# Output projection in one-tile steps, and a new order of all steps, in a two-branch attention and convolution kernel

## The chip, the cores and the metric

The kernel runs on one core of one Trainium2 chip. The time is device microseconds of one launch. TensorE (PE) does the matmuls, VectorE (DVE) and ScalarE (ACT) the elementwise work and the copies out of PSUM, GpSimd (POOL) tables and a few DMAs, and SyncE (SP) issues nearly all DMAs, in the order of the program.

## The reference, cut to what matters

Two independent branches over 2048 positions and 576 channels, joined along the last axis. A is attention with 32 heads of 18 channels, in which each position sees itself and seven earlier ones at distances 2, 4 up to 14, followed by a projection with `wo`. B is a short convolution of `k`, a product with `v`, a long causal convolution by FFT, and a product with `q`.

```python
qkv = (x @ wqkv).reshape(B, S, 3, H, Dh)          # A
logits = einsum("bhsd,bhswd->bhsw", q, kg) * scale # kg: k at s, s-2 ... s-14
o = einsum("bhsw,bhswd->bhsd", softmax(logits), vg)
a = o.reshape(B, S, D) @ wo
kv = (sum of 4 shifted k * shift_k) * v            # B
y = irfft(rfft(kv, 2 * S) * rfft(ssm_k, 2 * S))[:S] + kv * ssm_D
b = q * y
return concatenate([a, b], axis=-1)
```

## The kernel before

All work is cut into small steps, and a string `ORDER` lists them: the program issues them in exactly this order, and each engine works off its instructions in this order. An entry is a step's name with its indices. After a colon, "a" or "b" picks the PSUM pool of the step and "v" or "s" the engine that copies its result out of PSUM (DVE, L104, or ACT, L102; ACT if nothing is said). Each of the two pools has two tiles of two banks, so four tiles are in flight.

Branch A: `lx` loads x (L237), `xt` transposes it (L371), `lwq` and `lwt` load the weights, `qk` and `qt` project to q and k (L377), `lm` multiplies q by a shifted k on DVE (L493, L497), `lb` sums the products over a head (L502 to L510), `sm` is the softmax in seven parts per half of the positions, 0 to 6: maxima (L524 to L528), subtraction (L530), exp on ACT (L532), sum on PE (L536) with its logarithm and exp on ACT, normalising product (L540). `sp` spreads the result over partitions by DMA (L546), `v` projects to v (L384), `vh` copies its halo, `pm` multiplies v by the weights on DVE (L600), `ps` sums the products on PE (L610). `lwo` loads `wo` (L271), `po` is the output projection (L622, store L631), and `pz` a projection step that also holds the last two sums.

Branch B: `lk`, `lv`, `lkn`, `ld` are loads, `cv` the parts of the short convolution on DVE (L455 to L468), `kt` transposes the long filter (L481), `sx` and `kp` are the first FFT stage of the data and of the filter (L432), whose results go to DRAM (L439). `xl` and `kl` load them back in another layout (L559) into a ring of four slots; `xs` and `ks` are the second stage (L553), each with two PSUM tiles of one pool and two copies. `gp` multiplies the spectra on DVE (L575), `gi` is the first inverse stage (L588), stored to DRAM by POOL (L593). `yl` loads that (L649, the same ring), `ql` loads q (L653), `ys` is the last stage (L662) with the product by q on DVE (L666), and the result is stored (L668). `ia`, `ib`, `im` and the `t` entries make tables, `sk` and `wt` spread or reorder weights.

One `po.hv.r.di` takes a quarter of the positions' rows and half of the output columns. It holds two PSUM tiles, one of each pool, for the two blocks `e` of 128 positions; 36 matmuls alternate between them, and two copies and two stores follow.

Of the kernel before, what the change touches and what calls it, by code (L numbers as in the profile page):

```python
# [23 lines left out]
kp.7.1:a qk.0.0.1:b cv.1.0 cv.0.7 cv.1.5 kp.7.2:a cv.1.1 cv.2.3 sx.0.0:b kt.3:as qk.0.1.2:b wt:v cv.1.2 sx.0.1:av
cv.1.6 sx.0.2:b qt.1:a sx.1.0:b sx.1.1:b qk.1.0.1:a lv.2 sx.1.2:b kp.5.0:a qt.3:b qk.1.1.0:a cv.2.1 cv.1.7 cv.2.4
cv.3.1 cv.2.0 qt.2:a kp.5.1:b cv.3.4 kp.5.2:bv qk.0.1.1:a ia.5 cv.2.2 sx.2.0:av sx.2.1:b sx.2.2:bv lv.3 kt.0:as
sx.3.0:a sx.3.1:b cv.2.5 qk.1.1.1:b sx.3.2:a kp.3.0:a qk.1.1.2:b cv.3.3 kp.3.1:a ia.4 qt.0:b ib cv.2.6 cv.3.5 kp.3.2:a
ia.7 kt.4:bs cv.3.0 qk.1.0.2:a cv.3.2 kp.0.0:b cv.3.6 cv.2.7 kp.0.1:b cv.3.7 ia.2 kp.0.2:a kt.6:as lm.0.1 lm.0.2 ia.1
qk.0.0.3:b sx.4.0:a sx.4.1:b sx.4.2:a v.6:b lm.0.0 lm.1.0 lb.0:a ia.0 lm.1.1 sx.5.0:b sx.5.1:b lm.6.1 lm.6.2 sx.5.2:a
v.0:a lb.1:a sx.6.0:b sx.6.1:b vz sx.6.2:a lm.6.0 lm.7.1 ia.3 v.7:a lm.2.2 sx.7.0:b sx.7.1:a lb.6:b sx.7.2:a lm.7.0  # L30
v.8:b kp.4.0:a lm.2.0 kp.4.1:b lb.7:b lm.2.1 lm.3.0 kp.6.0:a xl.5 xl.2 kp.4.2:a kp.6.1:b v.2:b kp.6.2:a lb.2:a lm.3.1
lm.4.0 xs.5.0:b kl.2 xs.5.1:a kl.5 v.5:b lb.3:a lm.4.2 lm.4.1 xs.2.0:b im.1 v.1:a xs.2.1:b lm.5.0 lb.4:a lm.5.1
# [16 lines left out]
def kernel(  # L49
# [50 lines left out]
    def evac(dst, src, scale=None, on="s"):  # L100
        if (how["ev"] or on) == "s":
            nc.scalar.activation(dst, src, ACT.Copy, **({} if scale is None else {"scale": scale}))  # L102
# [455 lines left out]
    def w_load(Dd, key, i):  # L558
        nc.sync.dma_start(Wr.get((key, i)), by_rt(Dd, i // 4, i % 4))  # L559
# [65 lines left out]
    def p_fin(pss, hv, r, di):  # L625
        d0, d1 = DCH[di]
        for e in range(2):
            stage = sAr.get((hv, r, di, e))
            evac(stage, pss[e][:, :, 0:HD])
            a = 4 * (2 * r + e) + 2 * hv  # L630
            nc.sync.dma_start(outt[:, a:a + 2, d0:d1], stage)  # L631
            sAr.drop((hv, r, di, e))
# [82 lines left out]
```

## Time and profile before

| what | value |
|---|---|
| runs | 207.99, 210.42, 212.53 us, median 210.42 |
| profiled execution | 207.84 us, span 205.8 us |
| mean granted TensorE clock | 0.996 |
| PE busy, instructions | 189.4 us (92%), 2250 |
| DVE busy, instructions | 181.8 us (88%), 159 |
| ACT busy, instructions | 163.9 us (80%), 249 |
| all copies by ACT from psA and psB | 82.6 and 84.5 us, 237 of them |

How to read the profile. Times are microseconds, unless marked ns. The profile shows one execution; the span runs from its first to its last instruction, and the execution's own time is a little longer. PE is TensorE's matmuls, PEld its weight loads, SPq the issuing of DMAs by SyncE. L12 is line 12 of the kernel. In a timeline each row has the start, the duration from the first instruction's start to the last one's end, the engine, the line, the operation with its output and input, and the count; in brackets stands how long the engine was idle before it and what ended the wait. PEclk is the granted clock as a share of the full one. "psA" and "psB" are the two PSUM pools, "area" any of the SBUF areas.

The busy digits of the page, in 40 slices of the span, in tenths:

```profile
PE   7899989999999999999988897888999999999991
PEld 2564455544544666656746654556676777786871
DVE  6866999999999799999999997999999988994370
ACT  3799566999879988788798999989999995452352
```

Every engine is close to full from about 20 us on; ACT and DVE thin out in the last sixth.

### The profile page before, as it was taken

The numbers are of one execution on the slowest core, as the hardware profiler recorded it, in microseconds if no ns is written. First come the engines' busy times: TensorE is split into PE (matmuls) and PEld (weight loads), VectorE is DVE, ScalarE is ACT, GpSimd is POOL, SyncE is SP. The second block draws the span as 40 slices with busy tenths as digits, with TensorE's granted clock in tenths as the row PEclk, the third lists the DMA queues.
The fourth block names the chain that finished last, engine by engine and source line by source line (L and its number), as shares of the span: only waits on it lengthen the run. The fifth ranks groups of instructions, "written<-read, shape, count | busy, mean of one in ns | idle before, by whom it ended". The sixth has DMA issues, their size and how long they took to land.

```text
span 205.8 us, 5415 instructions
## 1 busy us (share of the span) xinstructions
PE 189.4 (92%) x2250; PEld 123.4 (60%) x2257; DVE 181.8 (88%) x159; ACT 163.9 (80%) x249; POOL 12.5 (6%) x39
## 2 busy tenths in 40 slices
PE   7899989999999999999988897888999999999991
PEld 2564455544544666656746654556676777786871
DVE  6866999999999799999999997999999988994370
ACT  3799566999879988788798999989999995452352
POOL 8300000000000000000020021001001011000000
PEclk9999999999999999999999999999999999999998
DMA  5999998876586874559897679999586998999866
GB/s 151 341 349 244 422 394 270 216 210 205 141 259 149 234 186 122 140 151 350 248 292 252 212 196 273 331 349 380 200 270 227 283 255 289 296 335 268 264 185 202
DMA packets 55162, 52.17 MB, mean 254 GB/s; under 512 B 7073, under 2 KB 49762, under 8 KB 55138
## 3 DMA queue, kind: packets, MB, share of 16 engines
q1 hardware_dynamic: 53888, 47.09, 76.8%
q0 software_dynamic: 1248, 4.74, 6.0%
q8 instruction: 17, 0.28, 0.6%
q14 instruction: 7, 0.06, 0.1%
q10 hardware_dynamic: 2, 0.00, 0.0%
HBM read 29.71 MB, written 18.87 MB: 236 GB/s over the span
## 4 chain that ended last, share of the span: by engine, by line
PE 48%; ACT 20%; DMA 14%; DVE 9%; issue 4%; SPq 3%; ACTq 1%; DVEq 0%
ACT area L102 19%; PE psB L384 6%; PE psA L622 5%; PE psB L622 4%; DMA area<-in_B_k_dram 4%; PE psB L610 4%; PE psA L384 3%; DMA area<-in_B_ssm_k_dram 3%; PE psA L377 3%; PE psB L377 3%; PE psB L432 3%; DMA area<-in_A_x_dram 3%; PE psA L432 2%; DMA Dx<-area 2%; DVE area L104 2%
## 5 line engine op out<-in xcount | busy, mean ns | idle before, releaser
L102 ACT ACTIVATE area<-psA 128x576 bf16<-128x576 f32 (+8 forms) x118 | 82.6, 739 | 25.6 <-PE psA L622 8.3
L102 ACT ACTIVATE area<-psB 128x576 bf16<-128x576 f32 (+6 forms) x119 | 84.5, 752 | 9.4 <-PE psB L384 3.2
L600 DVE TENSOR_TENSOR area<-area,area 128x4096 bf16<-128x4096 bf16 x18 | 40.6, 2286 | 0.7 <-DMA area<-area 0.6
L493 DVE TENSOR_TENSOR area<-area 128x4096 bf16<-128x4096 bf16 x16 | 35.6, 2283 | 1.0 <-ACT area L102 1.0
L377 PEld LDWEIGHTS <-area 128*128 128x128 bf16 x160 | 15.6, 98 | 17.1 <-issue 0.2
L461 DVE TENSOR_TENSOR area<-area,area 128x2304 bf16<-128x2304 bf16 x16 | 21.1, 1351 | 1.6 <-DMA area<-in_B_k_dram 1.6
L575 DVE TENSOR_TENSOR area<-area 128x2304 bf16<-128x2304 bf16 x16 | 21.5, 1352 | 1.0 <-PE psB L553 0.8
L553 PEld LDWEIGHTS <-W 128*64 128x64 bf16 x256 | 13.7, 108 | 11.9 <-issue 10.1
L384 PEld LDWEIGHTS <-area 128*64 128x64 bf16 x180 | 17.6, 193 | 3.4 <-issue 2.3
L377 PE MATMUL psA<-area,area 128*128 128x512 bf16 x78 | 18.5, 379 | 0.2
L377 PE MATMUL psB<-area,area 128*128 128x512 bf16 x77 | 18.4, 379 | 0.2
L622 PE MATMUL psA<-area,area 64*128 64x288 bf16 x144 | 18.0, 283 | 0.4 <-ACT area L102 0.4
L622 PE MATMUL psB<-area,area 64*128 64x288 bf16 x144 | 17.9, 283 | 0.0
L610 PEld LDWEIGHTS <-ident 64*64 64x64 bf16 x576 | 15.2, 106 | 3.2 <-issue 2.8
L588 PEld LDWEIGHTS <-IAt 64*128 64x128 bf16 x256 | 12.5, 94 | 7.5 <-issue 3.7
L622 PEld LDWEIGHTS <-area 64*128 64x128 bf16 x288 | 14.2, 94 | 4.5 <-issue 0.9
L553 PE MATMUL psB<-area,W 128*64 128x288 bf16 x136 | 13.0, 291 | 3.4 <-ACT area L102 2.0
L455 DVE TENSOR_TENSOR area<-area,area 128x2304 bf16<-128x2304 bf16 x11 | 14.8, 1352 | 0.1
L432 PEld LDWEIGHTS <-T 128*128 128x128 bf16 x96 | 8.5, 98 | 9.7 <-issue 3.4
L610 PE MATMUL psB<-area,ident 64*64 64x256 bf16 x384 | 12.4, 271 | 0.2
L384 PE MATMUL psB<-area,area 128*64 128x512 bf16 x100 | 12.2, 388 | 0.2
L432 PE MATMUL psA<-area,T 128*128 128x384 bf16 x52 | 11.9, 327 | 0.2 <-DVE area L363 0.2
(114 smaller groups left out, 212.6 us busy)
## 6 DMA issues: line engine op xcount, KB each, us to landing
Dk<-area SPq DMA_DIRECT2D x16, 288.0 KB, 3.4
Dx<-area SPq DMA_DIRECT2D x16, 288.0 KB, 3.1
area<-Dx SPq DMA_DIRECT2D x8, 576.0 KB, 6.4
area<-Dk SPq DMA_DIRECT2D x8, 576.0 KB, 5.3
Dy<-area POOLq DMA_DIRECT2D x8, 576.0 KB, 5.3
area<-Dy SPq DMA_DIRECT2D x8, 576.0 KB, 5.7
area<-in_A_x_dram SPq DMA_DIRECT2D x8, 288.0 KB, 5.6
area<-in_B_k_dram SPq DMA_DIRECT2D x4, 576.0 KB, 8.0
```

The lines of the kernel that those rows point to most:

```text
L102: nc.scalar.activation(dst, src, ACT.Copy, **({} if scale is None else {"scale": scale}))
L377: nc.tensor.matmul(ps[:, u, :], w[:, kb, cols[u]:cols[u] + 128], xT[:, j, kb], start=(kb == 0), stop=(kb == 4))
L384: nc.tensor.matmul(ps[64 * s:64 * s + 64, aa, :], wv[:, kb, n:D:9], xT[:, 2 * s + aa, kb], start=(kb == 0), stop=(kb == 4), tile_position= ...
L432: nc.tensor.matmul(ps[:, ri, 0:384], T1[:, ri, :], sf[:, 384 * ch:384 * ch + 384], start=True, stop=not extra)
L455: nc.vector.tensor_tensor(dst, dst, src, ALU.add)
L461: nc.vector.tensor_tensor(dst, kfull[:, 4 * c + 3 - j:4 * c + 7 - j, :], skb[:, j, :].unsqueeze(1).to_broadcast([128, 4, D]), ALU.mult)
L493: nc.vector.tensor_tensor(prr.get((n, h)), q2[h], k2[h][:, :, o0:o0 + S], ALU.mult)
L553: nc.tensor.matmul(ps[64 * hp:64 * hp + 64, im, 0:HD], W2[:, im, 8 * g + 2 * prl + hp].rearrange("p l f -> p (l f)"), Wt[:, 2 * prl + hp, ...
L575: nc.vector.tensor_tensor(Pv, Xv.unsqueeze(2).to_broadcast([128, 2, 2, 2 * HD]), Kv.unsqueeze(1).to_broadcast([128, 2, 2, 2 * HD]), ALU.mult)
L600: nc.vector.tensor_tensor(Pr.get((hv, p)), vv, L2[:, hv].rearrange("p a n t -> p n a t"), ALU.mult)
L610: nc.tensor.matmul(ps[64 * b:64 * b + 64, r, 0:256], ident[g, g], P[g, n, :, 128 * b:128 * b + 128], start=(n == 0), stop=(n == W - 1), ti ...
L622: nc.tensor.matmul(pss[e][:, b, 0:HD], Os[hv][g, i, r, 128 * e:128 * e + 128], w[g, d0:d1], start=(i == 0), stop=(i == 8), tile_position=( ...
```

## The change

A projection step now has one tile: a fourth index `e` names the block of 128 positions, and the step has 18 matmuls, one copy and one store. `pz` still has two tiles, but now does the seven first products of one tile before those of the other, and finishes one tile before it starts the last two products of the other.

```diff
-    def p_acc(pss, hv, r, di, lo, hi):
+    def p_acc(ps, hv, r, di, e, lo, hi):
         d0, d1 = DCH[di]
         for i in range(lo, hi):
             w = wos[0][:, i] if i < 3 else wos[1][:, i - 3]
-            for e in range(2):
-                for b in range(2):
-                    g = slice(64 * b, 64 * b + 64)
-                    nc.tensor.matmul(pss[e][:, b, 0:HD], Os[hv][g, i, r, 128 * e:128 * e + 128], w[g, d0:d1],
-                                     start=(i == 0), stop=(i == 8), tile_position=(64 * b, 0))
+            for b in range(2):
+                g = slice(64 * b, 64 * b + 64)
+                nc.tensor.matmul(ps[:, b, 0:HD], Os[hv][g, i, r, 128 * e:128 * e + 128], w[g, d0:d1],
+                                 start=(i == 0), stop=(i == 8), tile_position=(64 * b, 0))
...
-    def p_out(hv, r, di):
-        pss = [psum("a", 2, 512), psum("b", 2, 512)]
-        p_acc(pss, hv, r, di, 0, 9)
-        p_fin(pss, hv, r, di)
+    def p_out(hv, r, di, e):
+        ps = psum("b" if e else "a", 2, 512)
+        p_acc(ps, hv, r, di, e, 0, 9)
+        p_fin(ps, hv, r, di, e)

     def p_tail(hv, r, di):
         pss = [psum("a", 2, 512), psum("b", 2, 512)]
-        p_acc(pss, hv, r, di, 0, 7)
+        for e in range(2):
+            p_acc(pss[e], hv, r, di, e, 0, 7)
         p_sum(hv, 7, psum("a", 2, 512), "s")
         p_sum(hv, 8, psum("b", 2, 512), "v")
-        p_acc(pss, hv, r, di, 7, 9)
-        p_fin(pss, hv, r, di)
+        for e in range(2):
+            p_acc(pss[e], hv, r, di, e, 7, 9)
+            p_fin(pss[e], hv, r, di, e)
```

The order is new from the first entry to the last, with new choices of pool and copying engine. The stretches that matter here are the loads at the start, the middle around the softmax and the end:

```diff
-lwt lx.3.0 lx.3.1 tj t0 wm.11:a lx.0.0 t2 lx.2.0 tv xt.3.2:a sk.2:a sk.1:b lx.2.1 xt.3.1:bs sk.0:b xt.3.0:bs xt.2.2:as
...
-ks.2.0:b xl.1 ks.2.1:a ks.5.0:b lb.5:a gp.2.0 sm.0.0 sm.0.1 sm.0.2 sm.0.3 ks.5.1:b xl.3 gp.2.1 vh.0 sm.1.0 sm.1.1 kl.3
-gi.2.0:b kl.1 ql.0 ql.2 sm.0.4 v.4:a ql.1 sm.0.5:a sm.1.2 sm.1.3 sm.0.6 vh.2 v.3:bv sm.1.4 ql.3 ks.1.0:a gp.5.0 sp.0.0
-lwo.1 sp.0.1 gi.2.1:b xs.1.0:a im.0:v sm.1.5:b ks.1.1:b gp.5.1 vh.1 gi.5.0:a xl.0 sm.1.6 xs.1.1:b gi.5.1:a gp.1.0
...
-ys.2.1:bs ql.5 yl.6 yl.4 ps.0.0:a ys.0.0:a ys.0.1:b yl.7 ys.3.1:a po.0.0.0 po.0.1.1 po.0.1.0 ql.7 yl.5 ql.6 pm.1.2
-pm.1.6 pm.1.1 ps.1.6:b pm.1.8 ps.1.2:a pm.1.7 ps.1.1:b po.0.0.1:v pz.1.0.0:s ys.7.0:as po.1.0.1:v po.1.1.1 ys.4.0:b
-ys.4.1:as ys.6.0:as ys.7.1:b ys.5.0:as ys.5.1:b ys.6.1:a po.1.1.0
+lx.1.0 lx.1.1 lx.2.0 lx.3.0 lx.3.1 lx.2.1 tj wm.11:b t0 t2 xt.1.2:as xt.1.1:bs xt.1.0:as xt.3.1:as t3 lwt lwq.1.0 t1
+lx.0.0 lx.0.1 xt.2.1:b tv xt.2.2:bs xt.2.0:as qk.1.0.1:a lwq.0.1 lwq.0.0 lwq.1.1 xt.0.2:b lk.0 xt.0.0:b xt.3.0:as
...
+xs.2.0:b lm.3.1 lm.4.0 lm.4.2 im.0 v.1:a xs.5.0:b lb.3:a lm.4.1 xs.2.1:b v.4:a vh.0 lm.5.0 lb.4:a lm.5.1 xs.5.1:a kl.5
+ks.2.0:b ks.2.1:a lb.5:b gp.2.0 xl.7 ks.5.0:a xl.1 vh.2 gi.2.0:b gp.2.1 xs.1.0:a sm.0.0 sm.0.1 ks.5.1:b sm.0.2 xl.3
+sm.0.3 sm.0.4 sm.1.0 ql.2 xs.1.1:av ql.0 sm.1.1 kl.1 kl.3 ql.3 gi.2.1:b sm.1.2 sm.1.3 sm.0.5:a ks.1.0:b sm.0.6 gp.5.0
+v.3:av sp.0.0 sm.1.4 gp.1.0 lwo.1 ks.1.1:b sm.1.5:a sp.0.1 gi.5.0:a gp.5.1 sm.1.6 gi.1.0:b gp.1.1 vh.1 xs.3.0:b
+ks.3.0:a kl.0 sp.1.0 gi.5.1:b gp.3.0 xs.3.1:a ks.3.1:a pm.0.5 xl.0 kl.4 pm.0.6 gi.1.1:b gp.3.1 ks.0.0:a pm.0.7
...
+gp.4.1 yl.2 po.0.0.0.0:b yl.0 po.0.0.1.0:a gi.4.0:b pm.1.1 po.0.1.0.0:av gi.4.1:b pm.1.2 po.0.1.0.1:a gp.6.1 ys.3.0:bs
+ys.3.1:bs ys.1.0:as ys.1.1:as ql.4 ps.1.1:b ps.1.6:a gi.6.1:bv po.0.0.1.1:a po.0.1.1.0:b pm.1.4 po.0.1.1.1:b pm.1.5
+ys.2.0:as ys.0.0:as ql.7 yl.6 ys.0.1:b ys.2.1:as ps.1.2:a ps.1.4:a ps.1.5:a po.0.0.0.1:b pm.1.7 ql.6 yl.5 yl.7 pm.1.8
+yl.4 ql.5 pz.1.0.0:s po.1.0.1.0:a po.1.1.0.1:av po.1.1.1.0:av ys.6.0:b ys.6.1:as ys.7.0:a ys.7.1:bs ys.5.0:a ys.5.1:bs
+ys.4.0:b ys.4.1:a po.1.1.1.1:bv po.1.1.0.0:a po.1.0.1.1:b
```

Copies now marked for DVE are sk.0, kp.7.1, sx.0.0, kp.5.0, kp.0.0, xs.1.1, v.3, gi.6.1 and four projection pieces; before they were qk.0.0.2, kp.2.2, sx.0.1, kp.5.2, sx.2.0, sx.2.2, v.3, wt, im.0 and two projection steps of two copies.

More of the change, by code (lines that the diff above doesn't have):

```diff
@@ L24 @@
[L24 to L32, printed above, removed]
-ks.2.0:b xl.1 ks.2.1:a ks.5.0:b lb.5:a gp.2.0 sm.0.0 sm.0.1 sm.0.2 sm.0.3 ks.5.1:b xl.3 gp.2.1 vh.0 sm.1.0 sm.1.1 kl.3
@@ new lines @@
+cv.0.5 kt.2:bs kp.1.0:b kp.1.1:a lv.1 kp.1.2:a t5 qk.0.0.1:b kt.7:b kp.2.0:a kp.2.1:a kp.2.2:b kt.5:bs cv.0.6 cv.1.1
+qk.1.0.2:a cv.0.7 kp.7.0:b kp.7.1:av lwv cv.1.5 cv.2.3 ld cv.1.2 qk.0.1.0:b kp.7.2:b qk.1.1.0:a ia.5 sx.0.0:bv kt.3:as
+cv.2.1 sx.0.1:b sx.0.2:a cv.1.6 qk.0.0.0:b kp.5.0:av qt.3:b cv.3.3 kp.5.1:a cv.3.1 kp.5.2:a cv.3.4 cv.1.7 lv.3 cv.3.5
+qk.1.1.3:b sx.1.0:a sx.1.1:b sx.1.2:a ia.4 qk.1.1.2:b cv.3.0 sx.2.0:a cv.2.4 sx.2.1:b cv.3.2 qk.1.1.1:a cv.2.5
+sx.2.2:b sx.3.0:a qk.0.1.2:b lv.2 cv.3.6 kt.0:a sx.3.1:b cv.3.7 qt.1:a sx.3.2:b kp.3.0:b ia.3 qk.1.0.0:a kp.3.1:a
@@ new lines @@
+kp.3.2:b cv.2.0 qk.0.0.3:b cv.2.2 vz ia.1 cv.2.6 ia.6 cv.2.7 kt.6:a kp.0.0:bv kp.0.1:a kp.0.2:b kt.4:as lm.0.0 lm.0.2
+lm.0.1 v.7:b lm.6.2 im.1 ib lm.1.0 ia.7 v.2:a ia.0 sx.4.0:a sx.4.1:b lb.0:b sx.4.2:a sx.5.0:a v.0:b lm.1.1 sx.5.1:b
+sx.5.2:a lb.1:b sx.6.0:a lm.6.0 lm.6.1 sx.6.1:b sx.6.2:b v.6:a lm.7.1 sx.7.0:b sx.7.1:a sx.7.2:a lm.2.2 lb.6:b lm.7.0
+kp.4.0:a xl.2 kp.4.1:a lm.2.0 v.5:b lb.7:a lm.2.1 kp.4.2:b kp.6.0:b xl.5 kp.6.1:a lm.3.0 v.8:b lb.2:a kp.6.2:a kl.2
+xs.2.0:b lm.3.1 lm.4.0 lm.4.2 im.0 v.1:a xs.5.0:b lb.3:a lm.4.1 xs.2.1:b v.4:a vh.0 lm.5.0 lb.4:a lm.5.1 xs.5.1:a kl.5
@@ new lines @@
+pm.0.8 sp.1.1 xl.6 gi.3.1:b gp.0.1 ks.7.0:a pm.0.3 gi.0.0:b ks.7.1:a gp.7.0 xl.4 gi.0.1:b lwo.2 ps.0.3:a ks.6.0:b
+ps.0.8:a xs.6.0:b pm.0.0 lwo.0 pm.1.3 xs.6.1:a gi.7.0:b pm.1.0 ps.1.3:a ps.0.0:a gp.7.1 lwo.3 pm.0.2 ks.6.1:b xs.4.0:a
+yl.1 ps.1.0:b pm.0.1 gi.7.1:a ks.4.0:b xs.4.1:a ps.0.2:b ps.0.1:a ks.4.1:b ql.1 gp.6.0 yl.3 gp.4.0 gi.6.0:a pm.1.6
+gp.4.1 yl.2 po.0.0.0.0:b yl.0 po.0.0.1.0:a gi.4.0:b pm.1.1 po.0.1.0.0:av gi.4.1:b pm.1.2 po.0.1.0.1:a gp.6.1 ys.3.0:bs
+ys.3.1:bs ys.1.0:as ys.1.1:as ql.4 ps.1.1:b ps.1.6:a gi.6.1:bv po.0.0.1.1:a po.0.1.1.0:b pm.1.4 po.0.1.1.1:b pm.1.5
@@ L618, in p_acc, with p_fin @@
             w = wos[0][:, i] if i < 3 else wos[1][:, i - 3]
-            for e in range(2):
-                for b in range(2):
-                    g = slice(64 * b, 64 * b + 64)
-                    nc.tensor.matmul(pss[e][:, b, 0:HD], Os[hv][g, i, r, 128 * e:128 * e + 128], w[g, d0:d1],
-                                     start=(i == 0), stop=(i == 8), tile_position=(64 * b, 0))
-    def p_fin(pss, hv, r, di):
-        d0, d1 = DCH[di]
[L627 to L632, printed above, removed]
-    def p_out(hv, r, di):
-        pss = [psum("a", 2, 512), psum("b", 2, 512)]
-        p_acc(pss, hv, r, di, 0, 9)
-        p_fin(pss, hv, r, di)
+            for b in range(2):
+                g = slice(64 * b, 64 * b + 64)
+                nc.tensor.matmul(ps[:, b, 0:HD], Os[hv][g, i, r, 128 * e:128 * e + 128], w[g, d0:d1],
+                                 start=(i == 0), stop=(i == 8), tile_position=(64 * b, 0))
+    def p_fin(ps, hv, r, di, e):
+        d0, d1 = DCH[di]
+        stage = sAr.get((hv, r, di, e))
+        evac(stage, ps[:, :, 0:HD])
+        a = 4 * (2 * r + e) + 2 * hv
+        nc.sync.dma_start(outt[:, a:a + 2, d0:d1], stage)
+        sAr.drop((hv, r, di, e))
+    def p_out(hv, r, di, e):
+        ps = psum("b" if e else "a", 2, 512)
+        p_acc(ps, hv, r, di, e, 0, 9)
+        p_fin(ps, hv, r, di, e)
     def p_tail(hv, r, di):
         pss = [psum("a", 2, 512), psum("b", 2, 512)]
-        p_acc(pss, hv, r, di, 0, 7)
+        for e in range(2):
+            p_acc(pss[e], hv, r, di, e, 0, 7)
         p_sum(hv, 7, psum("a", 2, 512), "s")
         p_sum(hv, 8, psum("b", 2, 512), "v")
-        p_acc(pss, hv, r, di, 7, 9)
-        p_fin(pss, hv, r, di)
+        for e in range(2):
+            p_acc(pss[e], hv, r, di, e, 7, 9)
+            p_fin(pss[e], hv, r, di, e)
     def y_load(i):
```

13 lines of the change are left out of this document (3 added, 10 removed).

## The prediction

> **What bounds the kernel now.** I read the busy times by stage first, because the page's shares (PE 92%, DVE 88%, ACT 80%) are means over stages with different limits. The cuts are the end of the last logit product on DVE (108.1 us), the end of the last gi.1.1 matmul (131.8), of the last gi.4.1 matmul (169.2) and of the last matmul (201.6).
>
> ```profile
> core 0: us, PE busy (x) PEld busy (x) DVE busy (x) ACT busy (x) POOL busy (x), PEclk, DMA share, GB/s
> 28.60:108.10 79.50, 76.93 (x624) 45.02 (x633) 78.03 (x55) 69.61 (x97) 1.61 (x3) 1.00 0.74 216
> 108.10:131.80 23.70, 20.61 (x244) 13.79 (x239) 21.10 (x21) 22.79 (x38) 1.80 (x3) 1.00 0.81 240
> 131.80:169.20 37.40, 34.38 (x679) 25.54 (x678) 36.63 (x23) 36.07 (x67) 2.70 (x5) 1.00 0.90 287
> 169.20:201.60 32.40, 31.96 (x542) 24.80 (x540) 23.72 (x25) 14.53 (x26) 0.53 (x1) 1.00 0.92 273
> 201.60:205.80 4.20, 0.00 (x0) 0.00 (x0) 0.00 (x0) 1.15 (x2) 0.00 (x0) 0.82 0.62 184
> ```
>
> Call them A (from 0), B, C, D and the tail. In A, PE and DVE are both full; in B no engine is, so a chain of dependences rules; in C DVE and ACT are full; in D only PE; the tail is copy and store. Next the timeline of B, for that chain.
>
> ```profile
> 109.69 0.69 DVE L524 TENSOR_TENSOR area<-area 128x1024 bf16<-128x1024 bf16 x1 [0.27 <-ACT area L102]
> ...
> 111.20 1.22 DVE L530 TENSOR_TENSOR area<-area,area 128x2048 bf16<-128x2048 bf16 x1
> ...
> 112.51 1.91 ACT L532 ACTIVATE area<-area 128x2048 bf16<-128x2048 bf16 x1 [0.37 <-DVE area L530]
> ...
> 116.47 1.23 DVE L540 TENSOR_TENSOR area<-area,area 128x2048 bf16<-128x2048 bf16 x1
> ...
> 117.76 2.44 SPq L546 DMA_DIRECT2D area<-area  x4
> ...
> 121.02 3.55 SPq L546 DMA_DIRECT2D area<-area  x4
> ...
> 127.63 2.29 DVE L600 TENSOR_TENSOR area<-area,area 128x4096 bf16<-128x4096 bf16 x1 [0.64 <-DMA area<-area]
> ```
>
> The first softmax (max, subtract, exp, normalise) takes 109.69 to 117.70; its result is spread by eight DMAs, and the first value product (pm) waits for their landing at 127.6. Then the line of the spectrum loads, because the new order moves them closer to their use.
>
> ```profile
> L559 SPq DMA_DIRECT2D area<-Dx x8: 319/358/676, 90.6 to 148.2; - x8
> L559 SPq DMA_DIRECT2D area<-Dk x8: 319/329/2070, 99.1 to 144.9; - x8
> ...
> DMA to landing us min/median/max: 3.8/5.8/8.7
> ```
>
> **The change part by part.** Where I speak of an engine's work, I add up the entries of the order, each at the distance from start to start of such rows in the timeline: on DVE a conv product 1.27 us (four in 5.16 from 46.13), lm and pm 2.2 (five in 11.21 from 175.11), gp 1.27, a copy 0.66 to 1.2; on PE qk 2.16, v 2.37, xs and ks 0.61, gi 1.09, ps 0.93, ys 0.49; on ACT a step of xs, ks or gi 1.06 (two copies), ps 0.49. Over the kernel this makes 182 us on PE before and after.
>
> *Pieces of one tile.* 288 projection matmuls stay 288. In the timeline 108 of them run from 173.98 to 180.70, 62 ns each, so a step of 36 is 2.2 us and one of 18 is 1.1. The old order alternates the tiles after each pair, the new one stays on one tile. g_inv already stays on one tile: its 16 matmuls at 167.09 give way to the next group at 168.08, 62 ns each; others take 1.09 us, 68 ns. I take 62; the other end costs 288 x 6 ns = 1.7 us. Sixteen copies remain sixteen (about 0.54 us apart on ACT, 0.66 on DVE). Only the last step shows alone: one copy and one store follow the last matmul instead of two of each (201.56, 202.11), so the tail goes from 4.2 to 3.7 (bounds 3.1 and 4.2).
>
> PEclk is 1.00 in stages A to D, with y steps of four matmuls that change their tile every 0.49 us. The Trainium skill, "TensorE: Matmul & The Clock Gate", section on PSUM-queue depth-cycling, speaks against smaller steps: it says that frequent short PE pauses between groups can make the clock swing between half and full; by it the 17.8 us of projection could cost up to 17.8 more. No row here shows it.
>
> *Engines of the copies.* By the ":v" and ":s" marks and the rows' distances, ACT work falls by 1.6 us and DVE work grows by 2.2 over the kernel: xs.1.1 and gi.6.1 (2.6 us on DVE), sk.0 (1.2), two x transposes and one k transpose move to DVE; qk.0.0.2 (1.2), one kp/sx copy, wt and im.0 leave it. In C this relieves ACT by 2.1 us, but DVE is as full there, so I count no gain.
>
> *Stage A, reordered.* The first conv product waits for lk.0 (17.32). One more 320 KB weight piece goes ahead of it; at the 301 GB/s of the first 40 us that is +1.1 us. From there to the last logit product DVE has 86.6 us of work instead of 88.1. But kt.1's copy is now due after six conv products instead of kt.2's after seven; the same 7.5 MB lie ahead of its load, which landed at 27.1, so DVE, free at 26.2, waits 1.5 us. It must then copy kt.6 and kp.0.0 directly ahead of lm.0.0; PE has 62.5 us of work up to kt.6; its lag (time less summed work) was 6.2 us at this step before, and 0.6 less as the new order stands less in the first 36 us, so kt.6 is there at 68.1, when DVE has been free for about 1.2. The last product then ends at 109.6 instead of 108.1: +1.5 (bounds -0.6 without these waits, +1.8 if PE sets it, whose work to that point grows from 76.2 to 78.0 in a stretch that took 81.2).
>
> *Stage B, reordered.* The last logits are copied at 111.6 (before 109.65). gp.2.1 (1.3 us) is put on DVE ahead of the maximum, and the subtraction ends at 115.1 instead of 112.4. Queued on ACT ahead of the exp are the copies of ks.5.0, gi.2.0, xs.1.0 and ks.5.1. xs.1.0 needs load xl.1, which waits for the slot that xs.5.1 frees at 107.3; before, 19 us lay between xl.1's issue (100.5) and its use (119.8), now three entries of the order. With the 6.2 us of the load issued at 103.8 it lands at 113.5, and ACT reaches the exp at 115.9: +0.8 behind the subtraction. Exp, sum and logarithm take 5.1 us more to the normalised result at 121.0 (before 117.7). Behind it SP holds four spread DMAs, then lwo.1, which waits for v.3's matmuls; v.3 is behind ks.1.0, whose load kl.1 (5.3 us from 114.8, when ks.5.1 frees the slot) lands at 120.1. So lwo.1 goes at 123.5, the second four at 124.1 to 126.6, and they land at 130 (3.4 us). pm waits also for gp.3.0 behind ACT's copies, at 131.6. gi.1.1 ends at 134.1 instead of 131.8. Term of B alone: +0.8.
>
> *Stages C and D.* From the first pm to the end of the last, DVE has 56.3 us of work (56.5 before, in 58.6 us: 2.1 idle). 131.6 + 56.3 + 2.1 = 190.0; before 186.2. Ahead of the last pm PE now does eight projection pieces instead of six: from 134.1 it has 50.9 us to the sum that needs this pm and, with the 5.1 us it lost in C, gets there at 190.1. So DVE and PE meet. Left on PE are then 0.95 (sum), 0.65 (DVE copy), 0.5, six pieces 6.7 and eight y steps 3.9: 12.7 instead of 15.4 before (186.2 to 201.6). 190.0 + 12.7 = 202.7, that is 3.8 later at the pm and 2.7 of it won back. yl.6 waits on SP for gi.6.1's store (about 184) and holds output stores and three loads behind it; they land by 195, their y steps begin after 195, so I count nothing (up to +2 if not).
>
> Sum: 202.7 + 3.7 = 206.4 against the span of 205.8: +0.6. The profiled execution took 207.84; the runs shown have a median of 210.42 (207.99 to 212.53), 2.6 above it. I put the +0.6 on the median: 211.0.
>
> **The rivals.** *Faster.* The loads and knots of A and B cost nothing: pm starts at 127.7, where the second spread lands as before, with 2.7 us more of DVE's other work behind it. Then 127.7 + 56.3 + 1.0 idle + 12.7 + 3.7 = 201.4, -4.4, a time of 206.0. For it: the load issued at 91.1 took 4.9 us, and projection steps stand among ACT-bound steps in C. Against it: six named waits would all have to vanish.
>
> *Slower.* The shortened distance of the spectrum loads. They took up to 8.1 us (issued at 100.5); PE stood 0.68 us for ks.5.0 at 107.07 for this cause. At 8.1, xl.1 lands 2.2 later and delays exp; kl.1 2.7 later, and with it v.3, lwo.1 and the second spread; pm starts at 136.5, and the end, tied to it by DVE's chain, is 4.9 later: 215.9. It decides from a landing of xl.1 after 113.5.
>
> *Not what it says.* Matmuls on one tile at 68 ns: 212.7. Within the forecast's bounds; the clock case would give some 229.
>
> **How the numbers follow.** About 2% is what a measurement of this kernel can tell from no change: faster is below 206.2, slower above 214.6. Forecast 0.46; load rival 0.27; clock, one-tile cost and waits of the order that I have not seen, together, 0.05; faster rival 0.22. That gives 0.22 faster, 0.46 same, 0.32 slower. The forecast's own bounds (A -2.1 to +0.3, tail -0.6 to +0.5, tile +1.7, yl.6 +2) give 208.3 to 215.5. Eight in ten takes the faster case with a little of the runs' spread (205) and the load case (217).
>
> **What would show it.** Right: DVE idle before the first kernel-transpose copy (1 to 2 us); the exp at 115 to 117; a PE wait at xs.1.0 for a DMA from Dx; first pm at 130 to 133; last pm ending 189 to 191; projection matmuls at 62 ns; one copy after the last matmul. Wrong: first pm before 129, or the last pm before 187 with PE full from there, means the faster case; pm after 134 the slower; PEclk under 1.00 the clock.

## The result, and the profile after

The changed kernel takes 210.69 us (median of 22 runs, 209.09 to 213.35), the one before 208.77 (22 runs, 207.47 to 212.53). The ratio is 1.0098 (95% interval 1.0071 to 1.0124): about 2 us slower, which is clear of the noise but less than 2%. The profiled execution took 211.05 us and has a span of 209.1 and a mean granted clock of 0.987; before, the span is 205.8 and the clock 0.996.

The busy times by stage, with the columns of the same view before; the cuts are the same events, as the changed kernel reaches them:

```profile
28.60:111.40 82.80, 80.86 (x647) 47.17 (x649) 79.81 (x54) 68.34 (x91) 1.61 (x3) 0.98 0.73 200
111.40:134.30 22.90, 18.79 (x235) 12.48 (x229) 21.21 (x22) 22.76 (x39) 1.80 (x3) 1.00 0.89 276
134.30:171.50 37.20, 34.64 (x682) 25.64 (x682) 37.10 (x22) 34.40 (x64) 2.17 (x4) 1.00 0.91 280
171.50:204.20 32.70, 30.78 (x540) 23.47 (x534) 24.26 (x28) 16.92 (x28) 1.07 (x2) 1.00 0.96 283
204.20:209.10 4.90, 0.01 (x2) 0.00 (x0) 0.00 (x0) 0.65 (x1) 0.00 (x0) 0.80 0.44 127
```

Stage A ends 3.3 us later than before; B and C win back 1.0 together (22.9 and 37.2 against 23.7 and 37.4), D loses 0.3 and the tail 0.7. Up to the last matmul, A is the only stage with a granted clock below 1.00. The timeline shows what happened there, at 26 to 36 us:

```profile
27.83 0.75 PE L482 MATMUL psA<-ident,area 128*128 128x128 bf16 x8 [1.44 <-DMA area<-in_B_ssm_k_dram]
28.61 0.76 DVE L364 TENSOR_SCALAR area<-psA 128x576 int32<-128x576 int32 x1 [2.30 <-PE psA L482]
...
31.16 3.25 PE L378 MATMUL psB<-area,area 128*128 128x512 bf16 x10
...
35.07 0.76 DVE L364 TENSOR_SCALAR area<-psB 128x576 int32<-128x576 int32 x1 [1.90 <-PE psB L482]
```

PE stands 1.44 us in the middle of kt.1's transposes, for the filter load. Behind it ten matmuls take 3.25 us that take 2.32 elsewhere; PEclk is 0.50 from 30 to 33 us. DVE waits for kt.1 and again for kt.7, together 4.2 us. The wait of PE for the filter at this place in the kernel before, and the clock in the change:

```profile
27.21 0.62 PE L481 MATMUL psA<-ident,area 128*128 128x128 bf16 x7 [0.33 <-DMA area<-in_B_ssm_k_dram]
```

```profile
30.00:33.00 3.00, 3.00 (x10) 1.23 (x9) 3.00 (x3) 2.48 (x4) 0.00 (x0) 0.50 0.87 169
```

The softmax in B:

```profile
115.75 1.23 DVE L531 TENSOR_TENSOR area<-area,area 128x2048 bf16<-128x2048 bf16 x1
...
117.33 2.05 ACT L533 ACTIVATE area<-area 128x2048 bf16<-128x2048 bf16 x1
...
121.37 1.23 DVE L541 TENSOR_TENSOR area<-area,area 128x2048 bf16<-128x2048 bf16 x1 [0.54 <-ACT area L539]
...
125.91 2.52 SPq L547 DMA_DIRECT2D area<-area  x4
...
130.62 1.36 DVE L576 TENSOR_TENSOR area<-area 128x2304 bf16<-128x2304 bf16 x1 [0.39 <-ACT area L103]
132.06 2.29 DVE L601 TENSOR_TENSOR area<-area,area 128x4096 bf16<-128x4096 bf16 x1
```

Counted from the last logit product (111.38) the exp starts 6.0 us later instead of 4.4 before, the first pm 20.7 instead of 19.5. And the end:

```profile
178.94 0.53 POOL L594 DMA_DIRECT2D Dy<-area  x1 [5.49 <-DVE area L105]
...
184.15 0.37 SPq L650 DMA_DIRECT2D area<-Dy  x1
...
188.67 4.59 SPq L650 DMA_DIRECT2D area<-Dy  x3
...
197.69 0.66 PE L663 MATMUL psA<-area,IB 128*128 128x288 bf16 x4 [1.44 <-DMA area<-Dy]
```

The store of the last inverse block (gi.6.1) is issued at 178.94; before, the last such store was at 170.41:

```profile
170.41 0.53 POOL L593 DMA_DIRECT2D Dy<-area  x1 [3.17 <-ACT area L102]
```

Four loads read what it writes. They go out at 184.15 and from 188.67 on, and PE waits 1.44 us for one of these (yl.7).

For the experiments one table serves: one profiled execution of each kernel, all in us. An end is the start of the last row of its kind in the timeline plus its duration. "+" counts from the column to the left; the tail goes to the end of the span.

```
kernel           ratio of times [95%]     first   last logit  last pm  last    tail
                                          conv    product     ends     matmul
before           1                        17.32   108.14      +78.18   +15.28  4.20
the change       1.0098 [1.0071, 1.0124]  18.45   111.38      +77.84   +15.00  4.88
e1 steps only    0.9978 [0.9934, 1.0022]  15.48   107.65      +78.71   +15.31  4.13
e2a              1.0119 [1.0055, 1.0182]  18.97   112.37      +78.14   +14.61  4.88
e2b              1.0143 [1.0083, 1.0204]  19.36   111.35      +78.42   +14.68  4.85
e5 start         1.0180 [1.0128, 1.0233]  18.99   111.32      +79.80   +14.12  4.76
e6 softmax       1.0216 [1.0150, 1.0281]  18.52   109.38      +81.23   +14.06  4.83
e8 copies        1.0183 [1.0135, 1.0231]  18.35   110.03      +79.89   +17.78  3.70
e4 loads         1.0069 [1.0019, 1.0119]  18.67   112.39      +79.05   +14.99  4.07
e7 loads         1.0116 [1.0066, 1.0166]  18.66   109.31      +78.43   +14.89  5.27
h1 old first     0.9982 [0.9934, 1.0029]  17.13   108.26      +78.33   +14.88  4.83
h2 new first     1.0145 [1.0059, 1.0231]  19.50   110.63      +81.43   +15.48  4.16
e9 gi.6.1 early  0.9994 [0.9955, 1.0034]  18.95   109.95      +78.51   +13.85  3.69
both             0.9985 [0.9947, 1.0023]  17.66   108.28      +79.86   +13.86  3.70
```

Each ratio is to runs of the kernel before on the same chip. The rounds of experiments ran on four chips (e1, e2a, e2b and e4; e5 to e8; h1, h2 and e9; "both"), and the change itself only in the first measurement, so an experiment is compared with the change through these ratios and through the profiles. The profile of e4 is of the slowest execution of its kernel, so only its waits and its clock are read.

### The profile page after: what moved, and what is told of

Read it like the earlier page. It is cut to its first block, busy times and chain, and to the rows that moved or that the text cites. A ratio compares the mean times of both kernels' runs of the same rounds, so it can differ in the third digit from the quotient of the medians.

```text
span 209.1 us, 5422 instructions
## 1 busy us (share of the span) xinstructions
PE 189.8 (91%) x2257; PEld 122.2 (58%) x2257; DVE 184.2 (88%) x163; ACT 163.7 (78%) x247; POOL 12.7 (6%) x39
## 4 chain that ended last, share of the span: by engine, by line
PE 55%; ACT 19%; DMA 16%; SPq 4%; issue 3%; DVE 0%; ACTq 0%; DVEq 0%
ACT area L103 16%; PE psB L378 8%; DMA area<-in_B_ssm_k_dram 7%; PE psB L385 5%; PE psA L378 4%; DMA area<-Dy 4%; PE psA L433 4%; PE psB L622 4%; PE psA L611 3%; DMA area<-Dx 3%; PE psA L385 3%; PE psA L622 3%; PE psB L433 3%; DMA area<-in_A_x_dram 2%; PE psB L611 2%
## 5 line engine op out<-in xcount | busy, mean ns | idle before, releaser
L103 ACT ACTIVATE area<-psB 128x576 bf16<-128x576 f32 (+7 forms) x120 | 83.7, 738 | 17.9 <-PE psB L378 5.6
L103 ACT ACTIVATE area<-psA 128x576 bf16<-128x576 f32 (+9 forms) x113 | 79.6, 744 | 20.3 <-PE psA L622 5.1
L378 PE MATMUL psB<-area,area 128*128 128x512 bf16 x100 | 24.1, 390 | 0.1
L554 PE MATMUL psA<-area,W 128*64 128x288 bf16 x128 | 12.5, 290 | 3.1 <-ACT area L103 2.3
L589 PE MATMUL psB<-area,IAt 64*128 64x288 bf16 x192 | 14.2, 284 | 0.4 <-issue 0.2
L378 PE MATMUL psA<-area,area 128*128 128x512 bf16 x60 | 13.9, 379 | 0.1
L433 PE MATMUL psA<-area,T 128*128 128x384 bf16 x52 | 12.9, 342 | 0.4 <-ACT area L103 0.4
L611 PE MATMUL psA<-area,ident 64*64 64x256 bf16 x416 | 13.1, 271 | 0.2
L105 DVE CAST area<-psA 128x576 bf16<-128x576 f32 (+2 forms) x9 | 8.0, 902 | 5.9 <-PE psA L622 5.2
L554 PE MATMUL psB<-area,W 128*64 128x288 bf16 x128 | 11.4, 291 | 1.4 <-DMA area<-Dx 0.8
```

What stands on the lines that cost most here:

```text
L378: nc.tensor.matmul(ps[:, u, :], w[:, kb, cols[u]:cols[u] + 128], xT[:, j, kb], start=(kb == 0), stop=(kb == 4))
L433: nc.tensor.matmul(ps[:, ri, 0:384], T1[:, ri, :], sf[:, 384 * ch:384 * ch + 384], start=True, stop=not extra)
L554: nc.tensor.matmul(ps[64 * hp:64 * hp + 64, im, 0:HD], W2[:, im, 8 * g + 2 * prl + hp].rearrange("p l f -> p (l f)"), Wt[:, 2 * prl + hp, ...
L589: nc.tensor.matmul(ps[:, hp, 0:HD], IAt[r, tab, 4 * g + 2 * hv + u, :], Pp[(i, hv)][r, n, u, :], start=(n == 0), stop=(n == 3), tile_posit ...
```

## The experiments

**The small steps alone.** My theory was that one-tile steps cost nothing and that the loss sits in three knots of the new order, places where several engines wait on each other: the start, the softmax, the end.

```diff
-po.0.0.0 po.0.1.1 po.0.1.0 ql.7
+po.0.0.0.0 po.0.0.0.1 po.0.1.1.0 po.0.1.1.1 po.0.1.0.0 po.0.1.0.1 ql.7
```

> The kernel before with its own old order, in which every two-tile projection step is replaced in place by its two one-tile halves (and pz does one tile after the other). Theory (one-tile steps cost nothing, the loss of the change sits in its new order): projection matmuls 61 to 62 ns apart, PEclk 1.00 in the last 35 us, last logit product ends at 108 +- 0.7 as before, one copy after the last matmul, tail 3.5 to 3.8 instead of 4.2; ratio to the kernel before 0.994 to 1.001. Rival (more and smaller steps cost PE time): 66 ns or more a matmul or PEclk under 1.00 there, last 35 us longer by 1 us or more; ratio 1.005 to 1.011.

The timeline of e1 at its end:

```profile
200.40 1.27 PE L622 MATMUL psB<-area,area 64*128 64x288 bf16 x18
...
201.48 1.32 SPq L630 DMA_DIRECT2D out_dram<-area  x2
201.76 0.65 ACT L103 ACTIVATE area<-psB 128x576 bf16<-128x576 f32 x1 [0.45 <-PE psB L622]
```

The last two steps start 1.11 us apart (199.29 and 200.40), 62 ns a matmul, PEclk is full throughout, and the interval of the ratio holds 1. The steps cost nothing that can be measured, so the new order is what costs. But the tail is 4.13, not 3.7: one copy less behind the last matmul brought 0.1 us.

**The knot at the start.** First DVE's order alone, then PE's too:

```diff
-lk.2 lk.3 kt.1:a lv.0 ia.2 cv.1.3 cv.0.2 cv.0.5
+lk.2 lk.3 cv.1.3 cv.0.2 kt.1:a lv.0 ia.2 cv.0.5
```

> The changed kernel, with the conv products cv.1.3 and cv.0.2 put on DVE ahead of the copy of kt.1; PE's order is unchanged, so PE still pauses 1.4 us for the filter load. Theory P (PE sets stage A; DVE's waits of 2.30 and 1.90 us only show PE's pause and its slower clock): DVE's wait at kt.1 falls under 0.3, but it waits again at a later transpose copy, PEclk still falls under 1.00 between 27 and 36 us in some executions, the last logit product ends at 110.5 to 111.4; ratio 1.007 to 1.011. Rival V (DVE's waits are the loss themselves): the waits are gone for good, the last logit product ends at 107.5 to 109; ratio 0.994 to 1.002.

```diff
-cv.1.3 cv.0.2 kt.1:a
+cv.1.3 cv.0.2 qk.0.0.1:b kt.1:a
...
-kp.1.2:a t5 qk.0.0.1:b kt.7:b
+kp.1.2:a t5 kt.7:b
```

> As the run before it, and the projection qk.0.0.1 (2.2 us of PE, its operands long there) also put ahead of kt.1, so that PE works while the filter load lands. Theory (the start's knot is the main loss): no PE pause over 0.5 us between 20 and 36 us, PEclk 1.00 there, granted clock of every execution 0.993 or more, DVE's waits at kt.1 and kt.7 together under 0.6 instead of 4.2, the last logit product at 107.5 to 109 instead of 111.4; ratio 0.994 to 1.002. Rival (what comes later sets the end, the earlier start only lengthens waits in the middle or the end): the last logit product is earlier but the last matmul is within 0.7 us of 204.2; ratio 1.006 to 1.011.

One row of DVE's timeline from each, of e2a and of e2b:

```profile
36.06 0.76 DVE L364 TENSOR_SCALAR area<-psB 128x576 int32<-128x576 int32 x1 [4.32 <-PE psB L482]
```

```profile
39.85 0.96 DVE L105 CAST area<-psA 128x768 bf16<-128x768 f32 x1 [2.12 <-DMA Dk<-area]
```

In e2a the wait at kt.1 shrinks from 2.30 to 0.34 us and comes back at kt.7, 4.32: theory P holds there, though the last logit product, at 112.37, is later than its range. In e2b the pause of PE and the fall of the clock are gone (PEclk 1.00, every execution 0.993 or more), as expected, and yet the last logit product ends at 111.35. The copy of kp.7.1 now waits 2.12 us for the filter stores, whose ring has two slots, and DVE began its first product 0.9 us later than in the change's profile. Neither case holds whole. So I undid everything at the start that I could name, with these edits on top of those of e2b:

```diff
-qk.1.0.1:a lwq.0.1 lwq.0.0 lwq.1.1 xt.0.2:b lk.0 xt.0.0:b xt.3.0:as
-sk.1:b tw xt.3.2:a qk.0.0.2:b sk.0:av lkn.1 sk.2:a cv.0.0
+qk.1.0.1:a sk.1:b sk.0:av sk.2:a lwq.0.1 lwq.0.0 xt.0.2:b lk.0 lwq.1.1 xt.0.0:b xt.3.0:as
+tw xt.3.2:a qk.0.0.2:b lkn.1 cv.0.0
...
-cv.0.7 kp.7.0:b kp.7.1:av lwv cv.1.5 cv.2.3 ld
+cv.0.7 lwv cv.1.5 cv.2.3 kp.7.0:b kp.7.1:av ld
```

> The changed kernel with every knot of the start undone: the three sk steps directly behind qk.1.0.1, the weight piece lwq.1.1 behind lk.0, cv.1.3, cv.0.2 and qk.0.0.1 ahead of kt.1, and kp.7.0 and kp.7.1 behind cv.2.3, so that DVE does not wait for the ring of filter stores as it did (2.12 us) in the run with only the conv products and qk.0.0.1 moved. Theory (DVE's idle time in stage A passes to the end): DVE idle between its first conv product and its last logit product falls from 5.25 us to 2.5 or less, the last logit product ends 90 to 91 us behind the first conv product (92.9 in the changed kernel, 90.8 in the one before), at 107.5 to 109, the last pm follows 77.5 to 78.3 later as now; ratio 0.994 to 1.003. Rival (stage A is set by PE, whose work up to that point is 1.9 us more than before, DVE only shows it): another wait takes the place, the last logit product still ends at 110.5 or later; ratio 1.006 to 1.014.

111.32 again. DVE's idle time in A is 4.7 us instead of 5.25, the wait for the store ring became one of 1.6 us at kt.1 and another at the copy of sx.0.0, both for PE; the first product of DVE starts at 18.99, behind the table products, although lk.0 was issued 0.8 us earlier; and the stretch to the last pm grew. The last logit product is the rival's case, a wait repaired at the start being handed to the next step; the ratio of 1.0180 is above both ranges.

**The softmax.**

```diff
-gi.2.0:b gp.2.1 xs.1.0:a sm.0.0 sm.0.1 ks.5.1:b sm.0.2 xl.3 sm.0.3 sm.0.4 sm.1.0
+gi.2.0:b sm.0.0 sm.0.1 sm.0.2 sm.0.3 sm.0.4 gp.2.1 xs.1.0:a ks.5.1:b xl.3 sm.1.0
...
-gi.5.1:b gp.3.0 xs.3.1:a ks.3.1:a pm.0.5
+gi.5.1:b xs.3.1:a ks.3.1:a pm.0.5 gp.3.0
```

> The changed kernel with the knot of the softmax undone: maxima, subtraction and exp directly behind gi.2.0, so that gp.2.1 (DVE) and the copies of xs.1.0 and ks.5.1 (ACT) stand behind them, and gp.3.0 behind the first pm. Theory (the softmax chain sets pm's start and this the end): subtraction 3.1 us after the last logit product plus its copy, exp ends 1.3 to 1.6 earlier against the last logit product, first pm 18.8 to 19.6 us behind it instead of 20.7, the last pm 76.3 to 76.8 behind it instead of 77.8; ratio 1.001 to 1.005. Rival (DVE's own work and ACT's copies set the stretch, the order inside it is free): the pm starts earlier, but from the last logit product to the last pm it takes 77.4 us or more; ratio 1.007 to 1.012.

A row of PE's timeline in e6:

```profile
116.61 1.23 PE L554 MATMUL psA<-area,W 128*64 128x288 bf16 x8 [2.70 <-ACT area L103]
```

The exp came earlier (4.7 us behind the last logit product instead of 6.0) and the normalising product later (12.4 instead of 10.0). The row says why: the copies of xs.1.0 now stand behind the exp and hold their PSUM tiles, so PE waits 2.70 us at xs.1.1, and the matmuls that sum the exps are behind it on PE. Behind this pause the granted clock is 0.50 as well, for about 3.4 us from 116.4 on, and the 16 matmuls of gi.2.1, which also stand ahead of the sum, take 2.10 us instead of 1.21. So the delay is the wait and the clock together. 1.0216 is worse than either of my cases.

```diff
-ql.2 xs.1.1:av ql.0
+ql.2 xs.1.1:a ql.0
...
-pm.1.1 po.0.1.0.0:av gi.4.1:b
+pm.1.1 po.0.1.0.0:a gi.4.1:b
...
-ps.1.6:a gi.6.1:bv
+ps.1.6:a gi.6.1:b
```

> The changed kernel with the copies of xs.1.1, gi.6.1 and po.0.1.0.0 on ACT instead of DVE: 3.6 us less on DVE and 3.1 more on ACT between the last logit product and the last pm. Theory (DVE's work sets the end of the pms, so the copies given to DVE cost): from the last logit product to the last pm 74.5 to 76 us instead of 77.8; ratio 0.999 to 1.004. Rival (ACT is full in stages B and C, 22.76 of 22.9 and 34.4 of 37.2 us, so its copies come later and the others wait for them): 77.3 us or more; ratio 1.007 to 1.013.

The rival again, with a ratio above its range: DVE has 2.8 us less work between the last logit product and the last pm (72.8 instead of 75.6), and yet takes 2.1 us longer. The copy of xs.1.1 now stands on ACT between the exp and its sum, and PE waits 1.67 us for it at the sum. Two rows of PE's timeline in e8:

```profile
118.62 1.58 PE L537 MATMUL psA<-area,ident 128*128 128x256 bf16 x8 [1.67 <-ACT area L103]
...
199.55 0.66 PE L663 MATMUL psA<-area,IB 128*128 128x288 bf16 x4 [2.13 <-DMA area<-Dy]
```

Behind each of the two waits the granted clock is 0.50 for about 3.4 us. So what these copies cost on DVE can't be read from this ratio; it shows only that ACT is no better place for them.

**The order of the last loads.**

```diff
-ys.2.1:as ps.1.2:a ps.1.4:a ps.1.5:a po.0.0.0.1:b pm.1.7 ql.6 yl.5 yl.7 pm.1.8 yl.4 ql.5
+ys.2.1:as yl.5 yl.7 yl.4 ps.1.2:a ps.1.4:a ps.1.5:a po.0.0.0.1:b pm.1.7 ql.6 pm.1.8 ql.5
```

> The changed kernel, with the loads yl.5, yl.7 and yl.4 put on SP directly behind the stores of ys.0.1 and ys.2.1, ahead of the store of po.0.0.0.1 for which SP stood 2 us. Theory (the end's knot is the order on SP): the loads are issued from 186 on instead of 188.7 to 193.3, land by 194, PE's wait of 1.4 us at ys.7.0 and ACT's of 1.95 us are gone or under 0.4, from the end of the last pm to the last matmul 13.0 to 13.6 us instead of 15.0; ratio 1.001 to 1.004. Rival (the DMA queue is full at the end, whatever the order): the issue of the loads takes 4 us again or the output stores behind them land later, the tail grows by what PE wins; ratio 1.007 to 1.012.

```diff
-ys.2.1:as ps.1.2:a ps.1.4:a ps.1.5:a po.0.0.0.1:b pm.1.7 ql.6 yl.5 yl.7 pm.1.8 yl.4 ql.5
+ys.2.1:as ql.6 yl.7 yl.5 ql.5 yl.4 ps.1.2:a ps.1.4:a ps.1.5:a po.0.0.0.1:b pm.1.7 pm.1.8
```

> As the run with the three loads moved, and the loads ql.6 and ql.5 moved with them, in the order of their use, since there DVE waited 2.3 us for ql.6. Theory (the end's knot is the order on SP): no wait of PE, ACT or DVE over 0.5 us for a load or a store behind the last pm, from the last pm to the last matmul 13.0 to 13.8 us instead of 15.0, tail 4.0 to 4.2 instead of 4.9; ratio 0.998 to 1.003. Rival (the DMA engines are full at the end, so that any order only moves the wait): 14.7 us or more to the last matmul again, with another load or store waited for; ratio 1.004 to 1.010.

A row of DVE in e4 and one of PE in e7:

```profile
200.51 0.76 DVE L667 TENSOR_TENSOR area<-psB,area 128x576 bf16<-128x576 f32 x1 [2.34 <-DMA area<-in_B_q_dram]
```

```profile
198.05 0.67 PE L663 MATMUL psB<-area,IB 128*128 128x288 bf16 x4 [1.34 <-DMA area<-Dy]
```

The loads moved ahead landed in time, and the one behind them was waited for instead: ql.6 in e4, yl.4 in e7. In e4 the three issues from 187.67 us take 6.14 together (2.39, 1.70 and 1.90 by themselves); most earlier ones take 0.4 to 0.6 each. With a DMA share of 0.96 in stage D of the change the order alone doesn't help: e7 comes out where the change does, and e4 is not apart from it.

**Which part of the order?** Since single repairs told so little, I crossed the two orders at gp.2.0, where they have done the same steps but for five.

For h1, against the old order:

```diff
-xs.2.0:b im.1 v.1:a
+xs.2.0:b im.1 im.0 v.1:a
...
 ks.2.0:b xl.1 ks.2.1:a ks.5.0:b lb.5:a gp.2.0
-sm.0.0 sm.0.1 sm.0.2 sm.0.3 ks.5.1:b
+xl.7 vh.2 gi.2.0:b gp.2.1 xs.1.0:a sm.0.0 sm.0.1 ks.5.1:b sm.0.2 xl.3 sm.0.3 sm.0.4 v.4:a vh.0
...
```

> A cross of the two orders: the old order up to gp.2.0 (stage A and the first lines of B), the new order from there on, with one-tile steps. At that point the two have done the same steps but for five: im.0 is put behind im.1, v.4 and vh.0 behind sm.0.4, and xl.1 and ks.5.0, which the old order has done, are left out of the rest. Theory (the loss of the change sits in its first part, up to the last logit product): last logit product at 107.5 to 108.3 us, from there to the last pm 77.8 to 79, then 14.6 to 15.3 to the last matmul and a tail of 4.1 to 5; ratio 0.996 to 1.003. Rival (the new rest loses as much, about 1.2 us at the softmax and 0.7 in the tail, and wins nothing back): from the last logit product to the last pm 79.5 us or more; ratio 1.006 to 1.013.

For h2, against the new order, with im.0, v.4 and vh.0 left out of the rest:

```diff
 ks.2.0:b ks.2.1:a lb.5:b gp.2.0
-xl.7 ks.5.0:a xl.1 vh.2 gi.2.0:b gp.2.1
+ks.5.0:a xl.1 sm.0.0 sm.0.1 sm.0.2 sm.0.3 ks.5.1:b xl.3 gp.2.1
...
```

> The opposite cross: the new order up to gp.2.0, then ks.5.0 and xl.1, then the old order, in one-tile steps. Theory (the loss sits in the first part): last logit product at 109.3 to 112.4 us as in all six executions of this part so far, from there on as before (78.2 to 78.8, 15.3, 4.2); ratio 1.006 to 1.016. Rival (it sits in the rest): the old rest makes the later start good, last pm at 186 to 187.3; ratio 0.996 to 1.003.

h1 does what the theory says: 108.26, then the new rest in 78.33 and 14.88; 0.9982 [0.9934, 1.0029], apart from the change's interval. So the 1% goes when the first part is the old one. h2 is less clean than its ratio: its first part ends late (110.63), but its seam, where the two orders are joined, costs too, since ks.5.0 and xl.1 come behind gp.2.0 there: the first pm follows 22.4 us behind the last logit product instead of 19.5. A row of PE's timeline in h2:

```profile
118.09 1.59 PE L537 MATMUL psA<-area,ident 128*128 128x256 bf16 x8 [2.54 <-ACT area L533]
```

Behind this wait, too, the granted clock is 0.50 for about 3.4 us. Only the first 110.63 us of h2 speak for the theory.

**The late block itself.** Not the order of the loads, but the store that they wait for:

```diff
-gi.4.0:b pm.1.1 po.0.1.0.0:av gi.4.1:b pm.1.2 po.0.1.0.1:a gp.6.1 ys.3.0:bs
+gi.4.0:b gp.6.1 pm.1.1 po.0.1.0.0:av gi.4.1:b gi.6.1:bv pm.1.2 po.0.1.0.1:a ys.3.0:bs
...
-ps.1.6:a gi.6.1:bv po.0.0.1.1:a
+ps.1.6:a po.0.0.1.1:a yl.6 yl.7
...
-ql.7 yl.6 ys.0.1:b ys.2.1:as ps.1.2:a
+ql.7 ys.0.1:b ys.2.1:as ql.6 yl.5 ql.5 yl.4 ps.1.2:a
...
-pm.1.7 ql.6 yl.5 yl.7 pm.1.8 yl.4 ql.5
+pm.1.7 pm.1.8
```

> The changed kernel with its last inverse block early: gp.6.1 directly behind gi.4.0 and gi.6.1 behind gi.4.1, so that its store is issued at about 175 us instead of 178.9, and the loads that read it (yl.6, yl.7, then yl.5, yl.4) and ql.6, ql.5 earlier on SP. Theory (the late block crowds the last loads into a time when the DMA engines are full; the two runs that only reordered them moved the wait): no wait for a load over 0.5 us behind the last pm, 13.1 to 13.9 us from the last pm to the last matmul instead of 15.0, tail 4.0 to 4.4 instead of 4.9; ratio 0.999 to 1.004. Rival (the output stores alone keep the DMA engines full, or PE has to do the work anyway): 14.6 us or more, ratio 1.006 to 1.013.

POOL's and SP's timeline in e9:

```profile
174.02 0.53 POOL L594 DMA_DIRECT2D Dy<-area  x1 [1.91 <-DVE area L105]
...
179.80 1.21 SPq L650 DMA_DIRECT2D area<-Dy  x2
...
187.05 0.69 SPq L650 DMA_DIRECT2D area<-Dy  x1
...
190.29 0.87 SPq L650 DMA_DIRECT2D area<-Dy  x1
```

The store is 4.9 us earlier, two of the loads run before the crowded time, and no engine waits for a load behind the last pm. 13.85 us to the last matmul and a tail of 3.69: 2.3 us less than in the change, and a ratio of 0.9994, apart from the change's interval. Here the theory holds, and the tail of 3.7 of the prediction appears, with a DMA queue that is not behind. The ratio may hold more than these 2.3 us: e9 has the change's start, yet none of its twelve executions has a mean clock of 0.990 or less, against nine of the change's 22. Whether the edit also took away falls of the clock at the end, like the one in e8, is not shown; each kernel has one profile.

The last run ("both") has the edits of h1 and of e9 together.

> The two repairs that worked, together: the old order up to gp.2.0 with the new one behind it, and the last inverse block and its loads early. Theory (the two losses lie in different stages and add up): last logit product at 107.5 to 108.5 us, 78 to 79 more to the last pm, 13.6 to 14.0 to the last matmul, tail 3.6 to 4.1, a span of 203 to 205; ratio 0.984 to 0.993, faster than both kernels. Rival (the one repair already won what the other can, since the end is set by the DMA engines or by PE's whole work): the last matmul within 0.7 us of the better of the two runs by itself; ratio 0.995 to 1.001.

The stages did what they did alone: 108.28 at the start, 13.86 and 3.70 at the end. But from the last logit product to the last pm it took 79.86 instead of 78.33 or 78.51, DVE being idle 3.9 us there instead of 2.7 or 2.9, and 0.9985 [0.9947, 1.0023] excludes the range that I expected (0.984 to 0.993). The five kernels with the change's own order in this stretch (the change, e2a, e2b, e5, e7) took 77.8 to 79.8 for it, so one profile does not tell whether the two repairs together slow the pms. This execution took 207.84 us, less than the median of its twelve (208.30), so it was not an unlucky one. Why the repairs don't add up stays open. No kernel here is measurably faster than the one before; e1, h1, e9 and this one equal it.

## Why the prediction was right, and where it was not

The forecast, no change that can be measured, held, and 211.0 stands beside 210.69. The nearness is luck: I put +0.6 us on a median of 210.42 of three runs, and the kernel before has 208.77 in 22, 1.65 less; the loss was 1.9, not 0.6, 1.3 more; and these two errors nearly cancel. In the profiled execution the span is 209.1 instead of the 206.4 forecast, step by step:

- *Pieces of one tile*: 62 ns forecast, 61 to 62 measured. The clock case did not come: PEclk is 1.00 from 111.4 to 204.2 us in the change. What the Trainium skill, "TensorE: Matmul & The Clock Gate", section "A second HAM failure mode: psum-queue depth-cycling", tells of pauses between groups does not show in this trace.
- *Stage A, reordered*: 109.6 forecast, 111.38 measured, +1.8. Its first figure was right for a wrong reason. The first conv product starts at 18.45 (18.4 forecast), but behind the copy of sk.0 and the table products on DVE, with no wait for lk.0, whose pieces had landed by 18.0 (the last to land was issued at 10.78 and took 7.2 us). The wait at kt.1 was named and is 2.30 instead of 1.5; kt.6's is 0.2 instead of 1.2; the wait of 1.90 at kt.7 and the fall of the clock were in no step. The bounds of this term, -0.6 and +1.8, were too narrow: the measured +3.2 lies outside. Nor do the parts that the prediction names (+1.1, -1.5, +1.5 and +1.2) add up to its +1.5 but to +2.3; it doesn't show the rest. Yet the size fits executions without the fall of the clock: five kernels with the same first part (e6, e7, e8, e9, h2) end the last logit product at 109.31 to 110.63, around the 109.6 forecast.
- *Stage B*: counted from the last logit product, the second spread is issued from 14.5 us on, as forecast to a tenth, though v.3 (120.91 to 123.2) did not hold lwo.1 at 125.19. gp.3.0 was sooner, and pm starts at 20.7 instead of 22.0. The prediction's reading that no engine is full in B is wrong by its own line: ACT is busy 22.79 of 23.70 us there (96%), as full as in C. What it counted on ACT, the copies queued ahead of the exp, does hold the exp back.
- *Stage C*: 57.2 from the first pm to the end of the last instead of 58.4: the work was right (56.6 against 56.3), the idle time that I carried over from before (2.1) was 0.5. The last pm ends at 189.22, 190.0 forecast.
- *Stage D*: 12.7 forecast, 15.0 measured. This is the step that failed: "yl.6 waits on SP for gi.6.1's store (about 184) and holds output stores and three loads behind it; they land by 195 ... so I count nothing (up to +2 if not)". The first half is exact (184.15). But I took for granted that three loads issued together land like one. They landed at 195.1, 197.6 and 199.3. On PE the eight y steps, counted at 3.9 us, take 5.64 in the change (195.09 to 200.73) and 4.02 in e9, where the loads are early. So the late loads are 1.7 of the 2.3 us. To the last matmul e9 wins only 1.15 of it, because PE begins the last sum 0.8 us behind the last pm there, against 0.3 in the change.
- *Tail*: 3.7 forecast, 4.88 measured. e1 shows that the copy saved counts for little (4.13); in e9 and in "both", with the loads early, the tail is 1.2 us shorter than in the change.
- *The rivals*: for the load rival xl.1 had to take 8.1 us (the prediction's own view has 8.7 as the longest of its line). It took 4.7, from 109.93 to 114.63, and PE waited 0.35 us for it at xs.1.0. It landed after the 113.5 named as a sign only because it was issued 2.6 us later than forecast. For the faster rival the first pm had to start at 127.7; it started at 132.06.

Errors: +1.8 (A), -2.6 (B and C), +2.3 (D), +1.2 (tail), together the 2.7.

Where the loss went can be said for DVE, which sets the end of the pms. From its first conv product to the last pm it has the same work in both kernels, 163.3 us (89.16 + 16.89 + 57.27 before; 87.68 + 18.97 + 56.63 after). It starts 1.1 us later, and is idle 1.8 us more (7.5 against 5.7: 3.6 more in A, 1.8 less later). That is the 2.9 us by which the last pm is late. Both parts lie in A, and h1, in which A is the old one, shows neither.

The table separates them further. From the first conv product to the last logit product the five executions with the unedited new first part and no fall of the clock there take 90.6 to 91.7 us, the four with the old first part (before, e1, h1, "both") 90.6 to 92.2: no difference. With the fall it is 92.9 and 93.4 (the change, e2a). What is left without the fall is the start: the first conv product begins at 18.35 to 19.50 instead of 15.48 to 17.66, and the last logit product ends 1.0 to 3.0 us later. That an earlier start alone would win this back is not shown: e5 tried and started at 18.99, and e1, which started 1.8 us before the kernel before with the same first part, reached the last logit product only 0.5 earlier.

The part of the clock can be estimated from the runs. Of the change's 22, thirteen have a mean clock above 0.990, with a median of 210.28 us. Of the nine others seven lie at 211.05 to 212.15, with a median of 211.87, and two above. So some 1.5 us of the loss are there without a lower clock, and some 1.6 more go with it; by an estimate, 3.4 us at half clock instead of full are 1.7 us of PE's time.

## What to carry to other kernels

When an order is full on three engines, as in this kernel, a wait seen in the profile is not a price that can be saved by itself: of the seven local repairs (e2a, e2b, e4 to e8) none won measurably against the change, and three (e5, e6, e8) lost more than the change. Cross the two orders at a point where they have done the same work, to find the stage first; then move the producer (here the last block's store), not its consumers. In a forecast, a load that is counted at nothing because it "lands in time" needs the time for all that is queued with it.
